# Stack loads in 80 pieces from a scratch in blocks of 512 tokens, issued by SP, and SP's stores placed later behind their data

## The chip, the cores and the metric

The kernel runs on one core of one Trainium2 chip. The core has five engines that run side by side: TensorE (PE, matmuls, with its weight loads shown as PEld), VectorE (DVE), ScalarE (ACT), GpSimd (POOL) and SyncE (SP, which here only issues DMAs). Each engine takes its own instructions in order and waits for others by semaphores. The metric is the device time of one execution in microseconds (us); lower is better.

## The reference

Two results are mixed by a gate that each token computes for itself. One is multi-head attention over 2048 tokens with 32 heads of 20 channels (width 640); the other is the real part of a two-dimensional Fourier transform, written as products with given matrices.

```python
qkv = (x @ wqkv).reshape(B, S, 3, H, Dh)          # S = 2048, H = 32, Dh = 20
scores = einsum("bhqd,bhkd->bhqk", q, k) * Dh ** -0.5
a = einsum("bhqk,bhkd->bhqd", softmax(scores), v) ... @ wo
y = Cr @ (x @ Dr.T) - Ci @ (x @ Di.T)             # seq and hidden DFT matrices
out = g * a + (1 - g) * y                         # g = sigmoid((x * gate_w).sum(-1))
```

All data are float32.

## The kernel before, in words

**Precision.** A float32 operand is split in two parts of a shorter format (`split`, lines 98 to 103: a rounded copy and the rest), and a product is made of three matmuls (`three`). Queries and keys are kept in both parts in a DRAM scratch, `qk_scr`, whose first index is the part, the second the channel (640 of q, 640 of k), the third the token.

**Attention.** Heads go in 16 pairs, and a pair has two *units* of 1024 queries each, so there are 32 units (`NU`). For each pair two tiles are loaded, the *stacks* `kst` and `qst`: for each head 60 rows of 2048 tokens, the parts of its 20 channels stacked so that one matmul of 60 rows sums the three products (key rows: first, second, first part; query rows: first, first, second part). There are two buffers of each stack, by the parity of the pair. Two more rows per head in `qst` hold minus the row maxima of the scores.

A unit takes 32 *steps*, and in each of them PE makes, for both heads, one "m" score (line 159: queries by 512 keys, of which DVE takes the maxima at line 161) and one "e" score (line 685: keys by 512 queries, with the maxima subtracted through the two extra rows, which ACT turns into exponentials at line 687). The m scores run `LEAD` = 41 steps ahead of the e scores. So the maxima of a unit are known about 9 steps before its first e score; then (`max_chain`) PE transposes them, DVE splits them into `m1` and `m2`, and two steps later SP issues four small DMAs that put them into `qst` (lines 201 and 202). The m scores of the next pair begin at step 23 of a pair's 64.

Four steps make a *cycle*, written out by the string `ORDER`: eight e and eight m scores (each for one head), 15 places `F` for filling work, and at its end the *burst* `B`. In the burst PE multiplies the exponentials with `v` (line 448, sixteen matmuls), and DVE and ACT read out finished tiles.

**Filling work.** It is the Fourier transform. First 64 tiles of the product with the hidden matrices (`hid_tile`, lines 301 to 310), 10 of them before the first burst, the others one a cycle; they are stored to `a_scr`. Then, from cycle 57 on, the product with the sequence matrices (`dft_step`, line 523): 56 units of 16 dft steps. For these POOL prepares the operands: it adds or subtracts two tiles of `in_cdft` (line 419) or of `a_scr` (line 433) where a product wants that, and splits them. Results are added into `y_scr` (`finish_y`).

**End of a unit.** The accumulated `av` is copied to `o` by ACT (line 455) and then divided by its sums in seven small stages, each placed a number of steps behind the unit's end: `store_l` and `load_l` bring the sums through DRAM into the tile `lc`, `recip` (DVE, line 468) inverts them, `store_r` and `load_r` spread them over the rows of `rb`, `norm` (POOL, line 478) multiplies, and `store_o` writes `o_scr` (line 486).

**Order.** The program is written in the order of steps, and each engine runs its instructions in that order. `at_step(i, f)` puts a DMA or an instruction at the start of step i (`begin`). SP issues nearly all DMAs from one queue; a DMA that waits for its data holds everything that stands behind it on SP. In program order each SP DMA also waits for the one eight places before it to land. POOL issues the stack loads between its arithmetic: `load_stack(p)` yields twelve DMAs, and `begin` places them two steps apart, from step 2 to step 24 of the pair before. For each head and each of three column ranges (all keys; first and second half of the queries) it makes one DMA of 40 rows, for two stacked parts, and one of 20 rows. Pair 0's stacks are loaded by POOL before the loop (line 357).

Buffers: `raw_tile` has three, shared by the hid tiles' results and the `in_cdft` loads; `o`, `lc` and `rb` have one each; `m1` and `m2` two each.

Of the kernel before, what the change touches and what calls it, by code (L numbers as in the profile page):

```python
# [10 lines left out]
F32 = mybir.dt.float32  # L11
R = mybir.dt.float32r
# [6 lines left out]
P = 128  # L19
S = 2048  # L20
D = 640
H = 32
DH = 20
# [35 lines left out]
def f32(ap):  # L59
    return ap.bitcast(F32)  # L60
# [3 lines left out]
def mix_kernel(ctx: ExitStack, tc: tile.TileContext, xa, wqk, wb, cdft, wo, out):  # L64
# [12 lines left out]
    ps_a = pools(name="ps_a", bufs=1, space=PSUM)  # L77
    ps_y = pools(name="ps_y", bufs=1, space=PSUM)

    qk_scr = dram.tile([2, 2 * D, S], F32, name="qk_scr")  # L80
    v_scr = dram.tile([NP, P, NS, VW], F32, name="v_scr")
    a_scr = dram.tile([2, 2, NS, P, HE], F32, name="a_scr")
    y_scr = dram.tile([NS, P, D], F32, name="y_scr")
# [40 lines left out]
    def v_tile():  # L124
        return work.tile([P, NS, VW], F32, name="v", bufs=2)

    def load_stack(p):
        kt, qt = kst[p % 2], qst[p % 2]
        u = S // 2
        for t, o, two, one, cs in ((kt, D, 0, 2, slice(0, S)), (qt, 0, 1, 0, slice(0, u)), (qt, 0, 1, 0, slice(u, S))):  # L130
            for h in range(2):
                r = (2 * p + h) * DH
                b = 64 * h
                rows = slice(o + r, o + r + DH)
                yield f32(t[b + two * DH : b + (two + 2) * DH, cs]), qk_scr[:, rows, cs]
                yield f32(t[b + one * DH : b + (one + 1) * DH, cs]), qk_scr[0, rows, cs]

    def q_unit(n):
        u = n % 2 * (S // 2)
# [5 lines left out]
    def at_step(i, fn):  # L145
        later.setdefault(i, []).append(fn)
# [43 lines left out]
    def max_chain(n):  # L190
        q = q_unit(n)
        pt = bank()[:16, :P]
        pe.transpose(pt, nms.pop(n), ident)
        m1 = small.tile([16, P], R, name="m1", bufs=2)
        m2 = small.tile([16, P], R, name="m2", bufs=2)
        split(m1, m2, pt, dve, dve)

        def rows():
            for h in range(2):
                b = 64 * h + KROWS  # L200
                sp.dma_start(f32(q[b : b + 1, :]), f32(m1[8 * h : 8 * h + 8, :]))
                sp.dma_start(f32(q[b + 1 : b + 2, :]), f32(m2[8 * h : 8 * h + 8, :]))

        if now[0] < 0:
            rows()
        else:
            at_step(now[0] + 2, rows)
# [49 lines left out]
    def qk_tile(c, t):  # L257
        w = wt[c]
        ps = bank()
        cs = slice(t * 512, (t + 1) * 512)  # L260
        for d in range(ND):
            three(ps, w[:, 0, d], w[:, 1, d], xs[:, 0, d, cs], xs[:, 1, d, cs], d == 0, d == ND - 1)
        st = pair_tile()
        split(st[:, 0].bitcast(R), st[:, 1].bitcast(R), ps, act, dve)
        stores.append((qk_scr[:, c * P : (c + 1) * P, cs].rearrange("z p c -> p z c"), st))
        flush(2)

    def mm_b(j, s, ps, n):
# [137 lines left out]
    def load_c(g):  # L406
        n, j = divmod(g, 2)
        n, t = divmod(n, HT)
        raws = []
        for i, (_, th, ri) in enumerate(PRODUCTS[n][0]):  # L410
            raw = apool[0].tile([P, 1024], F32, name="raw2", bufs=2) if i and apool else raw_tile()
            o = (2 * ri + j) * 1024
            sp.dma_start(raw, cdft[th * HT + t, :, o : o + 1024])
            raws.append(raw)

        def finish():
            c = cparts[g] = part_tile()
            if len(raws) > 1:
                pool.tensor_tensor(raws[0], raws[0], raws[1], op=ALU.add if PRODUCTS[n][0][1][0] > 0 else ALU.subtract)  # L419
            split(c[:, 0], c[:, 1], raws[0], pool, pool)  # L420

        return finish
# [28 lines left out]
            unit_end(i, n)  # L451

    def unit_end(i, n):
        o = pa.tile([P, 512], F32, name="o")
        act.activation(o, av, AF.Copy)
        lc = pa.tile([P, 16], F32, name="lc")
        rb = pa.tile([P, 512], F32, name="rb")

        q = pool if n == NU - 1 else sp

        def store_l():
            q.dma_start(l_scr[n], o.rearrange("(j r) c -> j r c", j=4)[:, DH])

        def load_l():
            q.dma_start(lc, l_scr[n].rearrange("j (a b) -> (j a) b", b=16))

        def recip():
            dve.reciprocal(lc, lc)

        def store_r():  # L470
            q.dma_start(r_scr[n].rearrange("j (a b) -> (j a) b", b=16), lc)

        def load_r():
            for j in range(4):
                q.dma_start(rb[32 * j : 32 * j + 32, :], r_scr[n, j : j + 1].to_broadcast([32, 512]))

        def norm():
            pool.tensor_tensor(o, o, rb, op=ALU.mult)  # L478

        def store_o():  # L480
            for qc in range(2):
                for h in range(2):
                    j = 2 * qc + h
                    t0 = (n % 2) * (S // 2) + qc * 512
                    r = (2 * (n // 2) + h) * DH
                    q.dma_start(o_scr[r : r + DH, t0 : t0 + 512], o[32 * j : 32 * j + DH, :])

        steps = (1, 4, 10, 12, 15, 23, 25) if n < NU - 2 else (1, 4, 10, 12, 15, 19, 21)
        for k, fn in zip(steps, (store_l, load_l, recip, store_r, load_r, norm, store_o)):
            if n == NU - 1:  # L490
                rest.append(fn)
            else:
                at_step(i + k, fn)
# [7 lines left out]
    def dft_step(g):  # L501
        n, t, s = g // NS // HT, g // NS % HT, g % NS
        if s == 0:
            new_y(0), new_y(1)
            outs[n, t] = []
            for _, th, hf in PRODUCTS[n][2]:
                tt = th * HT + t
                y = None
                if (tt, hf) in signs:
                    y = apool[0].tile([P, HE], F32, name="yt", bufs=4)  # L510
                    sp.dma_start(y, y_scr[tt, :, hf * HE : (hf + 1) * HE])
                outs[n, t].append(y)
        if s % 8 == 0 and g // 8 + 3 < 2 * UNITS:
            cfin.append(load_c(g // 8 + 3))
        if s % 8 == 4 and cfin and g // 8 + 2 < 2 * UNITS:
            cfin.pop(0)()
        c = cparts[g // 8]
        cs = slice((s % 8) * P, (s % 8 + 1) * P)
        a = at[n % 2, s]
        for z, (cz, az) in enumerate(((0, 0), (0, 1), (1, 0))):  # L520
            for h in range(2):
                r = slice(64 * h, 64 * h + 64)
                pe.matmul(yp[h][:, :HE], c[r, cz, cs], a[r, az], start=s == 0 and z == 0, stop=s == NS - 1 and z == 2)  # L523
            if z < 2:
                yield
        w = g % (HT * NS) - 16
        if n + 1 == len(PRODUCTS) and w >= 0:
            d, r = divmod(w, 8)
            if r == 0 and d < ND:
                wos[d] = raw_tile()[:, :D]  # L530
                sp.dma_start(wos[d], wo[:, d])
            if r == 5 and d < ND:
                raw = wos.pop(d)
                for h in range(2):
                    wos[d, h] = a_tile(1, 2 * d + h)
                    split(wos[d, h][:, 0], wos[d, h][:, 1], raw[:, h * HE : (h + 1) * HE], pool, pool)
        if s == NS - 1:
            m = apool[0].tile([P, HE], F32, name="m", bufs=2)
            y0, y1 = yp[0][:, :HE], yp[1][:, :HE]

            def read():
                act.activation(m, y0, AF.Copy)
                dve.tensor_tensor(m, y1, m, op=ALU.add)  # L543

            extras.append((now[0], read))
            for out_, y in zip(PRODUCTS[n][2], outs.pop((n, t))):
                extras.append((now[0] + 5, functools.partial(finish_y, out_, t, m, y)))
        yield

    def finish_y(target, t, m, y):  # L550
        sg, th, hf = target
        tt = th * HT + t
        if (tt, hf) in signs:
            pool.tensor_tensor(y, y, m, op=ALU.add if sg == signs[tt, hf] else ALU.subtract)  # L554
        else:
            signs[tt, hf] = sg
            y = m
        at_step(now[0] + 4, functools.partial(sp.dma_start, y_scr[tt, :, hf * HE : (hf + 1) * HE], y))

    preps = []  # L560

# [69 lines left out]
    def begin(i):  # L631
        now[0] = i
        n, s = divmod(i, 32)
        for fn in later.pop(i, ()):
            fn()
        if s % 2 == 0:
            flush()
        if s == 0 and n % 2 == 0:
            p = n // 2
            if p + 1 < NP:  # L640
                at_step(i + 6, functools.partial(load_v, p + 1))
                for j, args in enumerate(load_stack(p + 1)):
                    at_step(i + 2 + 2 * j, functools.partial(pool.dma_start, *args))
        if i < total:
            pts[n, s // 2, s % 2] = pair_tile()

# [145 lines left out]
```

## Time and profile before

| | us |
|---|---|
| three runs | 1954.08, 1959.92, 1956.54 (median 1956.54) |
| the profiled execution's own time | 1953.52 |
| its span, first to last instruction | 1951.7 |
| mean granted TensorE clock | 0.997 of full speed |

A line of the page's groups names the source line, the engine, the operation, what is written and read, and how often; `<-` before an engine or DMA is what ended a wait. "Idle" is the time in which an engine had nothing running just before an instruction. In a list of waits stand the total in us, how many, and the longest. In a timeline stand the start, the length, and in square brackets the idle time before. `SPq` and `POOL ... DMA_DIRECT2D` are the issues of DMAs, not the transfers.

The loop of cycles runs from about 270 us to 1873 us; before it come the projections, after it the output projection and the mix.

### The profile page before, as it was taken

The numbers are of one execution on the slowest core, as the hardware profiler recorded it, in microseconds if no ns is written. First come the engines' busy times: TensorE is split into PE (matmuls) and PEld (weight loads), VectorE is DVE, ScalarE is ACT, GpSimd is POOL, SyncE is SP. The second block draws the span as 40 slices with busy tenths as digits, with TensorE's granted clock in tenths as the row PEclk, the third lists the DMA queues.
The fourth block names the chain that finished last, engine by engine and source line by source line (L and its number), as shares of the span: only waits on it lengthen the run. The fifth ranks groups of instructions, "written<-read, shape, count | busy, mean of one in ns | idle before, by whom it ended". The sixth has DMA issues, their size and how long they took to land. (4 is left out here: it accounts for less than half of the span.)

```text
span 1951.7 us, 43695 instructions
## 1 busy us (share of the span) xinstructions
PE 1918.5 (98%) x17080; PEld 1375.4 (70%) x17080; DVE 1454.1 (75%) x2419; ACT 1211.8 (62%) x2337; POOL 1045.8 (54%) x975
## 2 busy tenths in 40 slices
PE   8999999999999999999999999999999999999999
PEld 7987767777775667666666666666666666666679
DVE  4144568889887888888888878888888887888323
ACT  4221147777776676666776766676766776776741
POOL 1210001111005989457469968995786789787512
PEclk9999999999999999999999999999999999999999
DMA  7763321212114584435356746664554565454355
GB/s 224 173 172 127 130 100 46 78 61 74 47 58 141 170 228 152 122 116 149 97 173 199 196 154 189 212 177 123 149 171 125 183 169 181 154 149 147 98 165 179
DMA packets 196414, 281.02 MB, mean 144 GB/s; under 512 B 73272, under 2 KB 137816, under 8 KB 194288
## 3 DMA queue, kind: packets, MB, share of 16 engines
q1 hardware_dynamic: 158992, 246.20, 40.8%
q0 software_dynamic: 37216, 32.03, 6.7%
q8 instruction: 134, 2.20, 0.5%
q14 instruction: 72, 0.59, 0.1%
HBM read 213.81 MB, written 63.70 MB: 142 GB/s over the span
## 5 line engine op out<-in xcount | busy, mean ns | idle before, releaser
L161 DVE TENSOR_REDUCE mx<-ps 128x1 f32<-128x512 f32 x2048 | 1287.4, 683 | 197.4 <-PE ps L159 178.8
L687 ACT ACTIVATE p<-ps 128x512 f32<-128x512 f32 x2048 | 1080.9, 598 | 443.4 <-PE ps L159 241.2
L159 PE MATMUL ps<-kst,qst 60*128 60x512 f32 x2048 | 776.1, 427 | 8.0 <-DVE mx L161 3.2
L685 PE MATMUL ps<-qst,kst 62*128 62x512 f32 x2048 | 700.7, 422 | 5.8 <-DMA qst<-m 4.2
L523 PE MATMUL yp<-a,part 64*128 64x320 f32 x5376 | 687.6, 309 | 0.1
L523 PEld LDWEIGHTS yp<-a,part 64*128 64x128 f32 x5376 | 593.7, 186 | 15.3 <-DVE m L543 0.3
L448 PE MATMUL av<-p,v 128*21 128x512 f32 x4096 | 494.4, 599 | 0.1
L685 PEld LDWEIGHTS ps<-qst,kst 62*128 62x128 f32 x2048 | 335.5, 185 | 215.2 <-DVE mx L161 181.9
L159 PEld LDWEIGHTS ps<-kst,qst 60*128 60x128 f32 x2048 | 364.5, 185 | 38.2 <-DVE mx L161 11.8
L103 POOL TENSOR_TENSOR part<-raw,part 128x1024 fp32r<-128x1024 f32 x112 | 267.2, 2386 | 9.0
L448 PEld LDWEIGHTS av<-p,v 128*21 128x21 f32 x4096 | 98.3, 100 | 226.8 <-issue 223.1
L301 PE MATMUL yp<-wb,xs 64*128 64x320 f32 x1920 | 237.4, 309 | 3.7 <-ACT raw L309 3.5
L301 PEld LDWEIGHTS yp<-wb,xs 64*128 64x128 f32 x1920 | 206.8, 187 | 8.9 <-ACT raw L309 4.1
L419 POOL TENSOR_TENSOR raw<-raw,raw 128x1024 f32<-128x1024 f32 x78 | 187.4, 2402 | 17.3 <-DMA raw<-in_cdft 11.8
L102 POOL CAST part<-raw 128x1024 fp32r<-128x1024 f32 x112 | 116.4, 1039 | 116.8 <-PE yp L523 87.4
L102 POOL CAST wb<-raw 128x966 fp32r<-128x966 f32 (+1 forms) x4 | 3.4, 856 | 215.8 <-PE ps L159 215.8
L554 POOL TENSOR_TENSOR yt<-yt,m 128x320 f32<-128x320 f32 x64 | 55.5, 878 | 111.3 <-DVE m L543 104.2
L478 POOL TENSOR_TENSOR o<-o,rb 128x512 f32<-128x512 f32 x32 | 41.4, 1294 | 134.5 <-DMA rb<-r_scr 73.7
L103 POOL TENSOR_TENSOR a<-araw,a 128x320 fp32r<-128x320 f32 x112 | 97.8, 873 | 9.0
L103 DVE TENSOR_TENSOR p<-ps,p 128x512 fp32r<-128x512 f32 x40 | 27.5, 691 | 94.1 <-ACT p L100 91.4
L106 PE MATMUL ps<-xs,part 128*128 128x512 f32 x200 | 80.2, 401 | 7.8 <-ACT xs L100 6.1
L100 ACT ACTIVATE p<-ps 128x512 fp32r<-128x512 f32 x40 | 23.7, 597 | 101.4 <-PE ps L108 101.4
(67 smaller groups left out, 1331.8 us busy)
## 6 DMA issues: line engine op xcount, KB each, us to landing
raw<-in_cdft SPq DMA_DIRECT2D x192, 512.0 KB
araw<-a_scr SPq DMA_DIRECT2D x192, 160.0 KB
qk_scr<-p SPq DMA_DIRECT2D x40, 512.0 KB
kst<-qk_scr POOLq DMA_DIRECT2D x32, 320.0 KB, 12.3
qst<-qk_scr POOLq DMA_DIRECT2D x64, 160.0 KB, 8.2
a_scr<-raw SPq DMA_DIRECT2D x64, 160.0 KB
yt<-y_scr SPq DMA_DIRECT2D x64, 160.0 KB
y_scr<-yt SPq DMA_DIRECT2D x64, 160.0 KB
```

The source lines that it names most:

```text
L102: e1.tensor_copy(dst1, src)
L103: e2.tensor_tensor(dst2, src, f32(dst1), op=ALU.subtract)
L106: pe.matmul(ps, st1, mv1, start=first, stop=False)
L159: pe.matmul(ps, q[b : b + KROWS, qt * P : (qt + 1) * P], k[b : b + KROWS, kc * 512 : (kc + 1) * 512], start=True, stop=True)
L161: return lambda: dve.tensor_reduce(mx[n][:, h, qt, kc : kc + 1], ps, axis=AX.X, op=ALU.max)
L301: pe.matmul(yp[h][:, :HE], xs[r, xz, d, cs], w[r, wz, d, :HE], start=d == 0 and z == 0, stop=d == ND - 1 and z == 2)
L419: pool.tensor_tensor(raws[0], raws[0], raws[1], op=ALU.add if PRODUCTS[n][0][1][0] > 0 else ALU.subtract)
L448: pe.matmul(av[32 * j : 32 * j + DH + 1, :], v[:, kt, h * (DH + 1) : (h + 1) * (DH + 1)], pp[qc][:, h, :], start=kt == 0, stop=kt == NS - 1)
L523: pe.matmul(yp[h][:, :HE], c[r, cz, cs], a[r, az], start=s == 0 and z == 0, stop=s == NS - 1 and z == 2)
L554: pool.tensor_tensor(y, y, m, op=ALU.add if sg == signs[tt, hf] else ALU.subtract)
L685: pe.matmul(pt, k[b : b + KROWS + 2, kt * P : (kt + 1) * P], q[b : b + KROWS + 2, qc * 512 : (qc + 1) * 512], start=True, stop=True)
L687: act.activation(pts[n, kt, qc][:, h], pt, AF.Exp, scale=float(DH) ** -0.5)
```

## The change

The scratch of queries and keys is laid out in blocks of 512 tokens, so that what one `qk_tile` stores is contiguous for each part. A stack is loaded in six DMAs, one for each head and each of the three stacked parts, of 20 rows by four blocks of 512 tokens (80 pieces of 2 KB each); queries are no longer loaded in halves. There are twelve such DMAs for a pair as before. Inside the loop they are issued by SP at steps 2 to 13 of the pair before, one a step; POOL still issues those of pair 0.

The seven stages at the end of a unit are placed later (the last two units keep their places), and `o` gets a second buffer; the store of `y_scr` comes eight steps behind the addition instead of four; the loads of `y_scr` come at dft step 8 of a unit, behind the `in_cdft` load of the same step, instead of at dft step 0 ahead of it. `m1` and `m2` have one buffer each instead of two.

```diff
-    qk_scr = dram.tile([2, 2 * D, S], F32, name="qk_scr")
+    qk_scr = dram.tile([2, 4, 2 * D, 512], F32, name="qk_scr")
...
     def load_stack(p):
-        kt, qt = kst[p % 2], qst[p % 2]
-        u = S // 2
-        for t, o, two, one, cs in ((kt, D, 0, 2, slice(0, S)), (qt, 0, 1, 0, slice(0, u)), (qt, 0, 1, 0, slice(u, S))):
+        for t, o, parts in ((kst[p % 2], D, (0, 1, 0)), (qst[p % 2], 0, (0, 0, 1))):
             for h in range(2):
-                r = (2 * p + h) * DH
-                b = 64 * h
-                rows = slice(o + r, o + r + DH)
-                yield f32(t[b + two * DH : b + (two + 2) * DH, cs]), qk_scr[:, rows, cs]
-                yield f32(t[b + one * DH : b + (one + 1) * DH, cs]), qk_scr[0, rows, cs]
+                r = o + (2 * p + h) * DH
+                for k, z in enumerate(parts):
+                    b = 64 * h + k * DH
+                    yield (f32(t[b : b + DH, :]).rearrange("r (t c) -> r t c", t=4),
+                           qk_scr[z, :, r : r + DH, :].rearrange("t r c -> r t c"))
...
-        m1 = small.tile([16, P], R, name="m1", bufs=2)
-        m2 = small.tile([16, P], R, name="m2", bufs=2)
+        m1 = small.tile([16, P], R, name="m1")
+        m2 = small.tile([16, P], R, name="m2")
...
-        stores.append((qk_scr[:, c * P : (c + 1) * P, cs].rearrange("z p c -> p z c"), st))
+        stores.append((qk_scr[:, t, c * P : (c + 1) * P].rearrange("z p c -> p z c"), st))
...
-        o = pa.tile([P, 512], F32, name="o")
+        o = pa.tile([P, 512], F32, name="o", bufs=2)
...
-        steps = (1, 4, 10, 12, 15, 23, 25) if n < NU - 2 else (1, 4, 10, 12, 15, 19, 21)
+        steps = (6, 10, 16, 23, 27, 34, 45) if n < NU - 2 else (1, 4, 10, 12, 15, 19, 21)
...
         if s == 0:
             new_y(0), new_y(1)
             outs[n, t] = []
+        if s % 8 == 0 and g // 8 + 3 < 2 * UNITS:
+            cfin.append(load_c(g // 8 + 3))
+        if s % 8 == 4 and cfin and g // 8 + 2 < 2 * UNITS:
+            cfin.pop(0)()
+        if s == 8:
             for _, th, hf in PRODUCTS[n][2]:
...
-        if s % 8 == 0 and g // 8 + 3 < 2 * UNITS:
-            cfin.append(load_c(g // 8 + 3))
-        if s % 8 == 4 and cfin and g // 8 + 2 < 2 * UNITS:
-            cfin.pop(0)()
...
-        at_step(now[0] + 4, functools.partial(sp.dma_start, y_scr[tt, :, hf * HE : (hf + 1) * HE], y))
+        at_step(now[0] + 8, functools.partial(sp.dma_start, y_scr[tt, :, hf * HE : (hf + 1) * HE], y))
...
                 for j, args in enumerate(load_stack(p + 1)):
-                    at_step(i + 2 + 2 * j, functools.partial(pool.dma_start, *args))
+                    at_step(i + 2 + j, functools.partial(sp.dma_start, *args))
```

## The prediction

> **What bounds the kernel now.** I read the page's head first, then the waits of PE, then PE's timeline by its marker, the sixteen `av` matmuls (L448) that close every cycle of four steps.
>
> ```profile
> span 1951.7 us, 43695 instructions
> ...
> PE 1918.5 (98%) x17080; PEld 1375.4 (70%) x17080; DVE 1454.1 (75%) x2419; ACT 1211.8 (62%) x2337; POOL 1045.8 (54%) x975
> ```
> ```profile
> PE ps L685 <- DMA qst<-m: 4.2, 2, 3.3
> ...
> PE ps L159 <- DMA qst<-qk_scr: 2.4, 1, 2.4
> ```
>
> PE is busy 98% of the span, and no store, no cdft load and no POOL product ever holds it. A transfer reaches PE in two ways only: through the stacks (`qst<-qk_scr`) and through the two rows of maxima (`qst<-m`). So the change can win only what these waits cost, with what hangs on them, and lose only where it makes a new one. The price of a wait is read from the distance of `av` bursts:
>
> ```profile
> 1124.88 1.91 PE L448 MATMUL av<-p,v 128*21 128x512 f32 x16
> ...
> 1133.93 0.89 PE L685 MATMUL ps<-qst,kst 62*128 62x512 f32 x2 [3.28 <-DMA qst<-m]
> 1134.75 3.01 PE L448 MATMUL av<-p,v 128*21 128x512 f32 x16
> ...
> 1142.02 1.91 PE L448 MATMUL av<-p,v 128*21 128x512 f32 x16
> 1148.12 1.91 PE L448 MATMUL av<-p,v 128*21 128x512 f32 x16
> 1154.44 1.92 PE L448 MATMUL av<-p,v 128*21 128x512 f32 x16
> ```
>
> From 1142.02 on two cycles take 12.42 us, so an undisturbed cycle is 6.21 and a step 1.55. The two cycles before took 17.14: **place A costs 4.7 us**, of which 3.28 is the wait; the rest is a slower PE behind it (its next burst 3.01 instead of 1.91).
>
> Why were the rows late? DVE had them ready; SP sends them in its order:
>
> ```profile
> 1121.05 0.28 DVE L103 TENSOR_TENSOR m<-ps,m 16x128 fp32r<-16x128 f32 x1
> ...
> 1114.39 0.38 SPq L635 DMA_DIRECT2D y_scr<-m  x1
> 1124.67 1.42 SPq L486 DMA_DIRECT2D o_scr<-o  x4
> ...
> 1127.83 0.68 SPq L201 DMA_DIRECT2D qst<-m  x1
> ...
> 1122.69 0.64 POOL L635 DMA_DIRECT2D qst<-qk_scr  x1
> 1123.34 1.30 POOL L478 TENSOR_TENSOR o<-o,rb 128x512 f32<-128x512 f32 x1
> ```
>
> SP issued nothing from 1114.8 to 1124.67: it stood at the store of `o`, which waited for POOL's `norm` (L478, done 1124.6), itself behind a stack DMA that POOL issues. The rows, ready at 1121.3, left at 1127.83. Place B is the same with the other transfer in front:
>
> ```profile
> 1615.00 1.91 PE L448 MATMUL av<-p,v 128*21 128x512 f32 x16
> 1622.04 0.76 PE L159 MATMUL ps<-kst,qst 60*128 60x512 f32 x1 [2.40 <-DMA qst<-qk_scr]
> 1624.69 2.10 PE L448 MATMUL av<-p,v 128*21 128x512 f32 x16
> ...
> 1637.89 0.77 PE L685 MATMUL ps<-qst,kst 62*128 62x512 f32 x2 [0.95 <-DMA qst<-m]
> 1638.59 1.91 PE L448 MATMUL av<-p,v 128*21 128x512 f32 x16
> ...
> 1613.42 1.15 POOL L635 DMA_DIRECT2D qst<-qk_scr  x2
> 1616.88 1.15 POOL L635 DMA_DIRECT2D qst<-qk_scr  x2
> ```
>
> Three cycles took 23.59 instead of 18.63: **place B costs 5.0 us**. POOL had come late to its stack DMAs (1613 to 1618, where PE wanted the first half at 1619.6). Place C goes through DVE, which stood before the reciprocal of `lc`:
>
> ```profile
> 892.90 1.91 PE L448 MATMUL av<-p,v 128*21 128x512 f32 x16
> 900.49 1.92 PE L448 MATMUL av<-p,v 128*21 128x512 f32 x16
> ...
> 897.94 0.25 DVE L468 RECIPROCAL lc<-lc 128x16 f32<-128x16 f32 x1 [1.33 <-DMA lc<-l_scr]
> ...
> 886.53 0.32 SPq L465 DMA_DIRECT2D lc<-l_scr  x1
> ```
>
> One cycle of 7.59: **place C costs 1.4 us**. The little `lc` load took 11.4 us to land, in the steps where the stack DMAs run.
>
> **The change part by part.** SP's own waits show what its queue is made of:
>
> ```profile
> SPq L462 <- ACT p L687: 166.8, 29, 9.2
> SPq L471 <- DVE lc L468: 149.5, 28, 10.4
> ...
> SPq L486 <- POOL o L478: 108.0, 25, 14.9
> ```
>
> *The later steps* (6, 10, 16, 23, 27, 34, 45 after a unit's end, y stores 8 instead of 4 steps behind). `store_l` now comes 5 steps (7.8 us) later than before, against a mean wait of 5.8 (166.8/29); `store_r` keeps 7 steps behind the reciprocal instead of 2, and `store_o` 11 behind `norm` instead of 2, that is 17 us where the longest wait was 14.9. So these 424 us of waits mostly go. Only what stands behind them counts: the rows of maxima at step 26 no longer have `store_o` (25) before them but `store_r` (23), long due. Place A returns, and the second wait in B. The second `o` buffer is what lets `store_o` reach past the next unit's end; `m1` and `m2` with one buffer are rewritten 32 steps later, and cost nothing.
>
> *The stack DMAs* move from POOL's steps 2 to 24 to SP's 2 to 13. The m-scores of the next pair begin 23 steps into a pair (LEAD 41 of 64), so the last one has 10 steps, 15.5 us, to land. What did they take?
>
> ```profile
> kst<-qk_scr POOLq DMA_DIRECT2D x32, 320.0 KB, 12.3
> qst<-qk_scr POOLq DMA_DIRECT2D x64, 160.0 KB, 8.2
> ...
> L201 SPq DMA_DIRECT2D qst<-m x64: 634/648/780, 233.8 to 1829.1; - x64
> ...
> L486 SPq DMA_DIRECT2D o_scr<-o x124: 277/325/1522, 356.7 to 1855.7; - x124
> ```
>
> Even at 12.3 us they are in time, so the first wait in B returns. SP's issue of a 20x4x512 piece is not in the trace: between 0.33 (20 rows) and 0.65 us (the slow form), 4 to 8 us a pair of 99 us. I take 0.5, nearer to the 20-row store; it lies in the time that SP stood waiting, and were that used up, SP would run late by those 8 us, still inside 15.5. The first of them waits for PE's last e-score of the pair before, two steps earlier in program order; behind it stand SP's araw and cdft loads, which POOL wants 12 us later. POOL loses 12 issues a pair, which hides behind PE either way.
>
> The 80 pieces of 2 KB carry the same bytes. [...]
>
> *The order of y and cdft loads* at a unit's start: y now comes 8 dft steps later, half a unit (11 us) before its use by POOL. No cost while the half unit before POOL's use covers it; were that used up, POOL would wait, and PE not before POOL were a part behind.
>
> *The head.* Pair 0's stacks stay on POOL. There its ninth issue waited for the first to land, and the memset of `v` behind it held ACT and then PE:
>
> ```profile
> 73.05 1.19 POOL L357 DMA_DIRECT2D qst<-qk_scr  x2 [8.72 <-DMA kst<-qk_scr]
> ...
> 70.00:80.00 10.00, 7.36 (x50) 7.09 (x50) 0.56 (x1) 2.16 (x5) 3.57 (x6) 1.00 0.59 170
> ```
>
> PE lost 2.6 us in that stretch. Smaller first copies land earlier or not: 0 to 2.6 gained, I take 1.3.
>
> *From the hid tiles to the dft* two waits of ACT pass to PE:
>
> ```profile
> 596.05 0.44 ACT L309 ACTIVATE raw<-yp 128x320 f32<-128x320 f32 x1 [1.52 <-POOL raw L419]
> ...
> 611.93 0.44 ACT L309 ACTIVATE raw<-yp 128x320 f32<-128x320 f32 x1 [3.37 <-POOL raw L419]
> ```
>
> They hang on two cdft loads at steps 202 and 210, where SP now also issues pair 4's stacks (194 to 205) while POOL no longer does. The first may land later, the second earlier: between 4.9 gained and 4.9 lost, I take 0.
>
> *The new risk* is the `lc` load: its step 10 lies among the stack DMAs, and DVE's reciprocal stands 6 steps (9.3 us) behind it, as before. Bounds: 0, and place C's 1.4 at each of 15 pair starts, 21 us. I take one, 1.4, since before, with the same 6 steps, it happened once (the 8.7 of the next rows is after the last m-score, where DVE has time).
>
> ```profile
> DVE lc L468 <- DMA lc<-l_scr: 10.3, 3, 8.7
> ...
> 686.00:707.00 21.00, 21.00 (x209) 14.25 (x211) 17.88 (x30) 14.70 (x28) 16.90 (x21) 1.00 0.99 259
> ```
>
> **The sum**, against the profiled execution's own 1953.5 (span 1951.7 and 1.8 around it): minus 4.7, 5.0 and 1.4, minus 1.3, plus 1.4, gives 1942.5. That execution is 3.0 under the median of the runs shown, 1956.54, and these spread over 5.8. I can't see how much of that is waits of this kind, and go to the middle of 1942.5 and 1945.5: **1944 us**.
>
> [...]
>
> **The rivals.**
> *The waits only move* (chance 0.18). SP stays one queue, and its araw and cdft loads wait for buffers that POOL frees; in a heavy product POOL runs 6.6 us behind (`norm` at step 23 lies 9 steps, 14 us, before the first e-score of the next unit, wanted at 1130.65, so it was due at 1116.7 and ran at 1123.34). A late POOL then holds the rows through a load instead of a store. For it: SP had such waits already. Against it: the loads ask for buffers given back a cycle earlier, the store asked for work 2 steps old. If A and B come back: 1944 + 9.7 = 1953.7, no change.
>
> *Slower: DVE waits at every pair start* (0.15). Twelve stack DMAs in 17 us instead of 34, in one queue with `lc`. In the quoted 21 us of a pair start the DMA engines are 0.99 busy at 259 GB/s, and a stack is 1.92 MB, 7.4 us at that rate. It decides once `lc` takes over 9.3 us, and 11.4 was seen once. Price: 15 times 1.4, in place of the one in my sum: 1944 + 19.6 = 1963.6. Against it: only one of 15 pair starts had it, with POOL's DMAs running just then.
>
> *The change doesn't do what it says* (0.03): stacks land after step 23 because SP is late. Then B's wait recurs and eats A's gain, 1956.
>
> **Chances and range.** My forecast has 0.64, with a range of its own of 1939 to 1950. A measurement of this kernel can tell about 0.3%, 5.9 us: faster is below 1950.6, slower above 1962.4. Faster: 0.64 and a little of the first rival, 0.65; the same 0.19; slower 0.16, the second rival and a little. The range for 8 in 10 leaves out the slower rival (0.15) and a twentieth below: 1938, where the head and half of the 4.9 are won as well, to 1959.
>
> **What would show it.** Right: no wait of PE for `qst<-m` or `qst<-qk_scr`, L462, L471 and L486 gone from SP's waits, all DFT cycles between 6.1 and 6.5 us, and PE's clock at 1.00 there. Wrong: waits of DVE for `lc` at pair starts (second rival), PE waits at L685 or L159 with SP standing before L413 or L428 (first), a longer wait at L309 between 590 and 620.

## The result, and the profile after

The changed kernel takes **1933.69 us**, median of 6 runs (1931.83 to 1935.72); beside it the kernel before took 1960.32 (6 runs, 1954.08 to 1967.25). The ratio is 0.9869, 95% interval 0.9852 to 0.9885: faster by 1.3%. The profiled execution took 1935.29, 18.2 us less than that of before. Forecast were 1944 and a range of 1938 to 1959: the direction was right, the gain too small by half.

The page's head after, with PE's waits. The same PE work stands in a span that is 18.2 us shorter; both DMA rows (`qst<-m`, `qst<-qk_scr`) are gone, and so is the wait for `v` in the head.

```profile
span 1933.5 us, 43647 instructions
...
PE 1914.5 (99%) x17080; PEld 1374.1 (71%) x17080; DVE 1456.7 (75%) x2419; ACT 1211.5 (63%) x2337; POOL 944.3 (49%) x795
...
PE ps L106 <- ACT xs L100: 6.3, 1, 6.3
PE ps L158 <- DVE mx L160: 1.7, 2, 0.8
PE ps L106 <- ACT part L100: 1.3, 1, 1.3
```

PE's timeline after by its marker, first where place A was, then place B. The distances are 6.31, 6.09 and 6.17, then 6.13, 6.29 and 6.10: undisturbed cycles.

```profile
1111.38 1.92 PE L447 MATMUL av<-p,v 128*21 128x512 f32 x16
1117.69 1.91 PE L447 MATMUL av<-p,v 128*21 128x512 f32 x16
1123.78 1.92 PE L447 MATMUL av<-p,v 128*21 128x512 f32 x16
1129.95 1.91 PE L447 MATMUL av<-p,v 128*21 128x512 f32 x16
...
1602.20 1.91 PE L447 MATMUL av<-p,v 128*21 128x512 f32 x16
1608.33 1.92 PE L447 MATMUL av<-p,v 128*21 128x512 f32 x16
1614.62 1.92 PE L447 MATMUL av<-p,v 128*21 128x512 f32 x16
1620.72 1.92 PE L447 MATMUL av<-p,v 128*21 128x512 f32 x16
```

SP's own waits after: the longest sum is now at the rows of maxima, where SP is early and waits for DVE, as it should. What stood in its queue before, at the stores of `l`, `lc` and `o`, has fallen from 166.8, 149.5 and 108.0 to 52.7, 106.8 and 8.5.

```profile
SPq L200 <- DVE m L103: 253.5, 32, 13.3
...
SPq L470 <- DVE lc L467: 106.8, 19, 15.4
...
SPq L461 <- ACT p L687: 52.7, 22, 6.0
...
SPq L412 <- POOL raw L418: 35.3, 20, 5.9
SPq L427 <- POOL araw L432: 33.2, 17, 4.0
...
SPq L485 <- POOL o L477: 8.5, 1, 8.5
```

Where the 18.2 us came from, by the starts of the `av` bursts (256 cycles, numbered from 0; all numbers in us). "Before" was profiled four times in all, the first being the one that the prediction read; the other kernels are those of the experiments below.

| | before, four executions | after | places alone | stacks alone | store of `o` alone |
|---|---|---|---|---|---|
| span | 1951.7, 1951.9, 1954.1, 1956.3 | 1933.5 | 1933.7 | 1932.3 | 1949.6 |
| start of the first burst (head) | 279.1, 280.2, 280.6, 280.4 | 276.6 | 278.9 | 275.4 | 281.3 |
| cycles 48 to 63 (hid tiles to dft) | 106.6, 106.6, 109.3, 109.1 | 104.1 | 99.7 | 102.5 | 107.1 |
| cycles 96 to 103 (place C) | 51.2, 50.8, 50.3, 50.0 | 49.7 | 49.7 | 49.8 | 50.0 |
| cycles 128 to 135 (place A) | 54.6, 53.7, 52.4, 53.9 | 49.7 | 49.7 | 49.8 | 49.7 |
| cycles 208 to 215 (place B) | 55.2, 54.8, 56.0, 56.5 | 49.9 | 51.6 | 50.1 | 55.4 |

Against the first execution of before, from unrounded times: A 4.96, B 5.34 and C 1.49, together 11.8; the head 2.5; hid tiles to dft 2.5; and 1.5 in all other cycles, mostly the second cycle of each unit, which took 6.17 or more and takes 6.09 now. Its median is 6.09 to 6.10 in every run with the later places and still 6.17 with the stacks alone, so it belongs to the places; what shortens it is not known.

In the head the trace shows why. A line of a stretch has the time and the length, then the busy time and count of PE, PEld, DVE, ACT and POOL, the clock, the DMA share and GB/s. The window in which PE lost 2.6 us is full (before it held 7.36 busy), because POOL waits 3.6 us in short pieces for the first stack copies instead of 8.72 at one, and the memset of `v` behind them runs at 70.64 instead of 75.99. The other runs agree: where the stacks are loaded by copies of 20 rows, the first burst starts between 275.4 and 277.2, and where they are loaded by the old copies, between 278.9 and 281.3.

```profile
70.00:80.00 10.00, 10.00 (x70) 10.00 (x69) 0.83 (x1) 2.28 (x5) 1.91 (x3) 1.00 1.01 208
```
```profile
65.17 0.58 POOL L356 DMA_DIRECT2D qst<-qk_scr  x1 [0.48 <-DMA kst<-qk_scr]
66.39 0.58 POOL L356 DMA_DIRECT2D qst<-qk_scr  x1 [0.64 <-DMA kst<-qk_scr]
68.46 0.58 POOL L356 DMA_DIRECT2D qst<-qk_scr  x1 [1.49 <-DMA kst<-qk_scr]
70.06 0.58 POOL L356 DMA_DIRECT2D qst<-qk_scr  x1 [1.02 <-DMA kst<-qk_scr]
70.64 0.68 POOL L275 MEMSET v<- 128x672 f32 x1
```

From the hid tiles to the dft, SP's queue tells it, first of before, then of after. Before, the first pair of cdft loads stood behind `lc`'s load, which left 8.4 us behind the store of `l`, for whose landing it waited. That load now comes six steps later, and the cdft pair leaves at 581.93 instead of 587.28 and the next at 596.21 instead of 599.61 (of which 2.5 is the head).

```profile
576.87 0.54 SPq L462 DMA_DIRECT2D l_scr<-o  x1
585.24 0.31 SPq L465 DMA_DIRECT2D lc<-l_scr  x1
...
587.28 0.88 SPq L413 DMA_DIRECT2D raw<-in_cdft  x2
...
599.61 1.50 SPq L413 DMA_DIRECT2D raw<-in_cdft  x2
```
```profile
581.93 0.91 SPq L412 DMA_DIRECT2D raw<-in_cdft  x2
...
596.21 0.83 SPq L412 DMA_DIRECT2D raw<-in_cdft  x2
```

From issue to the start of POOL's work on it, the first pair takes longer now (8.3 us instead of 6.4), but the second, which had held PE longest, takes 5.6 instead of 10.0. It took 9.8 to 10.8 in all four executions of before and with the store of `o` alone, where POOL's old stack copies and the loads of `rb` are issued beside it; it takes 6.3 with the places alone, where `rb` comes later, and 6.1 with the stacks alone, where POOL issues no copies.

So the later places are not the only cure. With the stacks alone, where `lc`'s load kept its old place, it leaves 1.9 us behind the store, and cycles 48 to 63 take 102.5; with the store of `o` alone, where the old copies and the old place of that load stay, they take 107.1.

```profile
573.37 0.55 SPq L460 DMA_DIRECT2D l_scr<-o  x1
...
575.29 0.35 SPq L463 DMA_DIRECT2D lc<-l_scr  x1
```

The 2.5 us are a net gain: cycle 52 fell from 9.64 to 6.29, while cycle 54 rose from 6.07 to 7.65 through a lower clock (0.63, then 0.52; last section).

### The profile page after: what moved, and what is told of

Same layout as the page of the kernel before. It is cut to its first block, busy times and chain, and to the rows that moved or that the text cites. A ratio compares the mean times of both kernels' runs of the same rounds, so it can differ in the third digit from the quotient of the medians.

```text
span 1933.5 us, 43647 instructions
## 1 busy us (share of the span) xinstructions
PE 1914.5 (99%) x17080; PEld 1374.1 (71%) x17080; DVE 1456.7 (75%) x2419; ACT 1211.5 (63%) x2337; POOL 944.3 (49%) x795
## 5 line engine op out<-in xcount | busy, mean ns | idle before, releaser
L554 POOL TENSOR_TENSOR yt<-yt,m 128x320 f32<-128x320 f32 x64 | 55.4, 877 | 135.4 <-DVE m L543 128.3
```

## The experiments

**The places alone.** The changed kernel with the old scratch and the old 2 x 20-row and 20-row copies, issued by POOL at steps 2 to 24:

```diff
-                    at_step(i + 2 + j, functools.partial(sp.dma_start, *args))
+                    at_step(i + 2 + 2 * j, functools.partial(pool.dma_start, *args))
...
-    qk_scr = dram.tile([2, 4, 2 * D, 512], F32, name="qk_scr")
+    qk_scr = dram.tile([2, 2 * D, S], F32, name="qk_scr")
```

> The later places, the second o buffer and the y order of the change, with the stacks and their scratch as before (POOL, steps 2 to 24). If the gain of 26.6 us (1960.3 to 1933.7) comes from SP no longer standing before stores: 1938 to 1944, with no wait of PE for qst<-m, but head and hid-to-dft as before (first av burst near 279 us, a cycle of over 9 us between 600 and 615). If it comes from the stack transfers: 1950 to 1957.

Measured: 1937.06 us (1933.83 to 1942.65), ratio 0.9908 (0.9892 to 0.9925). A is gone. Of B its first wait is left, with one cycle of 7.90 (PE's timeline), and the head stays at 278.9.

```profile
1606.61 0.47 PE L160 MATMUL ps<-kst,qst 60*128 60x512 f32 x1 [1.58 <-DMA qst<-qk_scr]
```

**The stacks alone.** The kernel before with the new scratch and its 20x4x512 copies, issued by SP at steps 2 to 13; the old places and buffers stay.

> The scratch in blocks and the twelve loads of 20x4x512 from SP at steps 2 to 13, with all places of stores as before. If SP's standing before stores is the cause: 1950 to 1957, SP's waits at the store of o and at l_scr still over 80 us each, and late stacks or rows on PE. If the stack transfers are the cause: 1936 to 1942, first av burst near 276.6 us, no cycle over 9 us.

Measured: 1934.21 us (1933.86 to 1935.26), ratio 0.9887 (0.9875 to 0.9900). A, B and C are all gone, although the store of `o` still stands ahead of the rows. At place A POOL, which issues no stacks now, runs `norm` in time, and SP gets through (first POOL, then SP):

```profile
1109.78 1.29 POOL L476 TENSOR_TENSOR o<-o,rb 128x512 f32<-128x512 f32 x1
```
```profile
1111.10 3.08 SPq L484 DMA_DIRECT2D o_scr<-o  x4
...
1115.61 0.68 SPq L199 DMA_DIRECT2D qst<-m  x1
```

So the two parts overlap: savings of 19 and 22 us against the 1956.25 us that before took in that series, and no 41 together. This run changes both the shape of the copies and the engine that issues them; which of the two cures A at the old places was not tried.

**POOL issues the new copies.** The changed kernel, with `pool` in place of `sp` at `at_step(i + 2 + j, ...)`.

> All of the change, but POOL issues the twelve pieces of a pair, at the same steps 2 to 13. If only order on SP and the pieces' shape matter: 1933 to 1937, as with SP. If POOL's lateness in heavy products is what made stacks late: PE waits for qst<-qk_scr at pairs near 1100 and 1590 us, 1938 to 1948.

Measured: 1933.35 us (1932.75 to 1934.66), ratio 0.9883 (0.9870 to 0.9896). With these copies and the later places, it makes no difference which engine issues. Here the page shows the landing of all the new copies, from the key stacks' row and the query stacks':

```profile
kst<-qk_scr POOLq DMA_DIRECT2D x96, 160.0 KB, 6.3
qst<-qk_scr POOLq DMA_DIRECT2D x96, 160.0 KB, 7.9
```

**SP issues the old copies.** The changed kernel with the old scratch and the old copies, but on SP at steps 2 to 13.

> All of the change, but the scratch and the pieces as before (40 and 20 rows, queries in halves), issued by SP at steps 2 to 13. If the pieces' shape does not matter: 1933 to 1937. If the 40-row pieces run on few DMA engines and delay what stands beside them: 1938 to 1950, with the first av burst back near 279 us, DVE waiting for lc at pair starts or PE waiting for stacks.

Measured: **2090.48 us** (2086.92 to 2093.60), ratio 1.0685 (1.0667 to 1.0702). This is the prediction's slower rival in full size. The waits of DVE, PE and SP:

```profile
DVE lc L469 <- DMA lc<-l_scr: 128.8, 14, 12.6
```
```profile
PE ps L687 <- DVE mx L162: 63.2, 9, 10.4
PE yp L525 <- DVE m L545: 31.5, 3, 11.8
```
```profile
SPq L637 <- DMA kst<-qk_scr: 102.7, 31, 8.4
```

DVE stands at the reciprocal 14 times, 9.2 us in the mean (128.8/14), and PE behind it. Per pair of 15 the kernel loses 10.2 us ((2086.0 - 1933.5)/15), of which 0.3 is the later first burst.

**The same, with rows of 8 KB in copies of 20.** As the last one, but each copy loads 20 rows at full width from one part, as the changed kernel does. Beside the old scratch, the edit against the changed kernel is:

```diff
-                    yield (f32(t[b : b + DH, :]).rearrange("r (t c) -> r t c", t=4),
-                           qk_scr[z, :, r : r + DH, :].rearrange("t r c -> r t c"))
+                    yield f32(t[b : b + DH, :]), qk_scr[z, r : r + DH, :]
```

> The changed kernel, but with the old scratch layout: SP still issues twelve stack copies of 20 rows at steps 2 to 13, each row one run of 8 KB now instead of four of 2 KB. It tells the shape of a copy (20 rows in one level against 2 x 20 rows) from its pieces of 2 KB. Theory 1 (a copy of 2 x 20 rows is moved by few DMA engines and so lands late, and holds what is queued behind it; one whose slowest level has 20 rows is not): as the changed kernel, 1930 to 1938 us, stack copies landing in 6 to 8 us, and no wait of DVE for lc at pair starts. Theory 2 (the pieces of 2 KB in blocks of 512 tokens are what shortened the landing): as the kernel with 40-row copies on SP, 2050 to 2100 us, with DVE waiting for lc about 9 us at most pair starts.

Measured: 1935.27 us (1934.68 to 1939.04), ratio 0.9885 (0.9865 to 0.9905). The layout in blocks of 512 tokens and the 80 pieces are not what helps: this kernel has the old layout, is not told apart from the changed one, and stands 155 us below the last. The two differ only in how a stack is cut: there, six of the twelve copies of a pair go over both parts in one (and the queries in halves). What that does shows in stretches in which nearly all packets were rows of 8 KB, those of the stacks, first of the last kernel, then of this one:

```profile
498.00:500.00 2.00, 2.00 (x27) 1.95 (x25) 1.97 (x4) 1.85 (x4) 0.00 (x0) 1.00 0.13 53
500.00:502.00 2.00, 2.00 (x25) 1.71 (x26) 1.96 (x4) 1.41 (x4) 0.00 (x0) 1.00 0.13 53
```
```profile
476.00:478.00 2.00, 2.00 (x25) 1.89 (x21) 1.94 (x4) 1.57 (x4) 0.00 (x0) 1.00 0.68 176
```

A share of 0.13 is as much as two of the 16 DMA engines at work all the time, and 0.68 as much as about eleven. The six copies carry 1,280 KB a pair (two of 320 and four of 160); at 53 GB/s they need some 25 us, an estimate, where steps 2 to 13 are 17, and the load of `lc` is issued among them. No row names the engines, and why 53 GB/s moved in the first two stretches and 176 in the third is not shown.

How much of the harm is SP's and how much the faster pace is open: the places alone took 1937.06 us with the same copies, but there POOL issued them over steps 2 to 24, and SP was not tried at that pace.

**The store of `o` alone.** The kernel before with two edits that belong together:

```diff
-        o = pa.tile([P, 512], F32, name="o")
+        o = pa.tile([P, 512], F32, name="o", bufs=2)
...
-        steps = (1, 4, 10, 12, 15, 23, 25) if n < NU - 2 else (1, 4, 10, 12, 15, 19, 21)
+        steps = (1, 4, 10, 12, 15, 23, 45) if n < NU - 2 else (1, 4, 10, 12, 15, 19, 21)
```

> The kernel before, with one edit: the store of o at step 45 after a unit's end instead of 25, and the second buffer of o that this needs. The old scratch and the 40-row copies on POOL stay. If place A was the rows of maxima standing behind the store of o on SP, as the prediction read it, the wait of PE for qst<-m at cycles 128 to 135 goes and these eight cycles take 49.7 us instead of 54.6; place B keeps its first wait (qst<-qk_scr, 2.4 us) and loses its second (0.95), C keeps its 1.4, and head and hid tiles are as before: 4.7 + 1.0 less than the kernel before, a ratio of about 0.997. If the rows were late through the stack copies instead, the wait stays and the ratio is 1.000. If most of the gain of the later places comes from this one store (they alone gave 0.9908), the ratio is 0.991 to 0.993.

Measured: 1950.54 us (1945.87 to 1953.83), ratio 0.9961 (0.9949 to 0.9974), with before at 1957.71. A is gone (49.7), B is not (55.4, with a first wait of 3.83 us). This shows A's cause as the prediction read it: POOL's `norm` is as late as ever, and the rows of maxima leave 2.4 us before it, instead of behind it (SP, then POOL):

```profile
1122.76 0.68 SPq L201 DMA_DIRECT2D qst<-m  x1
```
```profile
1125.20 1.30 POOL L478 TENSOR_TENSOR o<-o,rb 128x512 f32<-128x512 f32 x1
```

**Before, three times more.**

> The kernel before, unchanged, for a second profiled execution. Its times ran from 1952 to 1967 us, those of the changed kernel from 1932 to 1936. If this spread is waits of the kind of A, B and C that come and go from one execution to the next, this trace shows the same kinds of waits at other units, and their cycles account for its difference from 1953.5 us. If the spread lies elsewhere (the clock, the ends of the span), A, B and C stand at the same cycles with the same lengths.

> The kernel before, unchanged, for one more profiled execution. In its 17 runs of the second series the time falls by 1.8 us for each 0.001 of mean granted clock (0.990 at 1964.94, 0.996 at 1953.41); two profiled executions, both near the short end, showed A, B and C at the same cycles. If a longer execution (over 1957) comes up and its extra time is a lower clock: the same waits of PE as in the first, with cycles at clock 0.83 in more places. If it is more waits: waits of PE for DMA well over 6.6 us in sum.

> The same as the one before it: the kernel before, unchanged, for a fourth profiled execution, to see where its time differs from the others. Expected if the clock is the cause: cycles with waits take longer than the wait in them, at clock 0.83, and the longer the execution the more of those; if more waits: waits of PE for DMA well over 6.6 us in sum.

Measured: 1953.65, 1958.07 and 1955.91 us. All four executions have A, B and the hid tiles' stalls at the same cycles (the table above; C in parts). The longest, 1956.3 of span, has its extra 4.6 us mostly there: 2.5 from the hid tiles to the dft, 1.4 in the head, 1.3 in B, and 1.4 in cycles 144 to 151, where the rows of maxima were late a third time; 0.8 and 1.1 less in A and C. PE's waits for DMA in it are 8.0 us, against 6.6 in the first:

```profile
PE ps L685 <- DMA qst<-m: 5.7, 3, 2.3
...
PE ps L159 <- DMA qst<-qk_scr: 2.3, 1, 2.3
```

So most of what varies is waits at the places that the prediction found, and the slower PE behind them (in the longest the burst behind A's wait of 2.30 us took 3.30 instead of 1.91). Executions over 1960 were not profiled, and stay open.

**The dft one cycle sooner.** After the change some cycles between hid tiles and dft are still long, so this was tried to beat it: the changed kernel with `first = start // 4 + 2` in place of 3.

> The changed kernel, with the dft starting one cycle sooner after the hid tiles (start // 4 + 2 instead of + 3), so that one cycle less runs without fills. Theory 1 (what is left of the slow cycles 50 to 56 is the empty cycles: PE idles behind ACT there and its clock falls to 0.83 at 630 to 640 us): one of the long cycles at 54 to 56 (7.7 against 6.2) goes, 1.0 to 3 us less than the changed kernel, 1931 to 1933. Theory 2 (the wait for POOL's raw, which waits for the in_cdft load, sets the place): the same loads are wanted a cycle sooner, the waits of ACT at L308 grow by as much, and the time is that of the changed kernel or up to 3 us more.

Measured: 1939.69 us (1937.73 to 1942.11), ratio 0.9905 (0.9885 to 0.9925). One 7.73 cycle became 6.32 as theory 1 has it, but the next takes 11.52: PE waits for POOL's `a`, because POOL works on without a gap (none over 0.1 us from 619.9 to 652.7) and can't be ready sooner. POOL sets that place, at another of its tiles than theory 2 said.

```profile
644.61 0.63 PE L523 MATMUL yp<-a,part 64*128 64x320 f32 x2 [2.53 <-POOL a L102]
```

**The cdft loads one cycle sooner.**

```diff
-            if c in (HID - 5, HID - 3):
-                at_step(i + 4, load_c((c - HID + 5) // 2))
+            if c in (HID - 6, HID - 4):
+                at_step(i + 8, load_c((c - HID + 6) // 2))
```

> The changed kernel, with the first two pairs of cdft loads issued one cycle (6.2 us) sooner on SP, and POOL's work on them left where it is. Theory 1 (between the hid tiles and the dft the changed kernel still waits because these loads land late: ACT stands at L308 for POOL's raw at 592.6, and cycle 50 takes 7.31): cycle 50 goes to 6.25, and cycles 48 to 63 together lose 1 to 4 us of their 104.1, 1930 to 1933 us. Theory 2 (the three raw buffers are the limit: two of them are held a cycle longer, so ACT stands there as long, or longer): cycles 48 to 63 take 104 us or more, and the time is that of the changed kernel or up to 3 us above it.

Measured: 1932.35 us (1930.26 to 1933.36), ratio 0.9875 (0.9856 to 0.9893); span 1930.5. Cycle 50 went from 7.31 to 6.24, and cycles 48 to 63 from 104.1 to 102.9: in this one execution it goes as theory 1 has it, with 1.2 us. Cycle 50 differs from run to run without this edit too (6.25 where POOL issues the new copies, 8.19 with rows of 8 KB). It is the shortest median of all kernels here, but its interval covers that of the changed kernel: not shown to be better.

## Why the prediction was right or wrong

The causes at A, B and C were read rightly, and the gain came out twice as large as forecast because the terms beside them were too small. The largest of these, the cycles from the hid tiles to the dft, was put at 0 and measured 2.5.

**Places A, B and C: right.** The sum took off 4.7, 5.0 and 1.4; 11.8 went against the same execution. "Place A returns" is shown for the later store by the store of `o` alone; what the prediction missed is that the new copies, issued by SP at the old places, return A as well, so A had two sufficient cures. For B's first wait the stack copies were named rightly: with places alone 1.58 us of it stays. C varies between 0.4 and 1.5 us over the four executions, and is 0.3 with the store of `o` alone; the sum took its high end from one execution, and what cures it is not settled. No run shows why its 1.4 should go, as the sum has it; the runs showed cycles 96 to 103 at 49.7 after the change and with the places alone, at 49.8 with the stacks alone and at 50.0 with the store of `o` alone, against 50.0 to 51.2 before. Two of the signs named for being right did not hold in full, without a cost: of the 424 us that SP stood at the three stores, 168 are left, most of them at the store of `lc` (106.8 us, longest 15.4), and single dft cycles still take 6.5 to 6.8 us.

**"Even at 12.3 us they are in time": true only with the change's own copies.** Twelve old copies on SP cost 153 us of span. The prediction weighed them as so many KB in one queue (7.4 us at 259 GB/s), and put the risk on the new copies, which by the runs are the safe ones (1934.21 us where SP issues them at the old places, 1933.69 in the change). The slower rival's mechanism, place and deciding point (an `lc` load over 9.3 us) were right; its cause was the shape of the copy, not the number in one queue. Its price of 1.4 for each pair start was taken from one mild case, and was 10.2 where it struck.

**The head: mis-sized.** 1.3 taken from 0 to 2.6; 2.5 measured, and against the four executions of before 3.5 (mean 280.1 against 276.6).

**From the hid tiles to the dft: this step failed.** "The first may land later, the second earlier ... I take 0": it measured 2.5 gained, and 3.8 against the four executions. The two directions were right for the landing (1.9 us longer for the first pair, 4.4 shorter for the second), but they were set off against each other to nothing. The reasoning also left out that the wait for `l`'s store, which held the first pair's issue, goes: by the prediction's own later steps, and, as the stacks alone show, by the new copies too. The opening had put the place aside already ("no cdft load and no POOL product ever holds it"), though the list of PE's waits before has it:

```profile
PE yp L301 <- ACT raw L309: 3.5, 2, 2.7
```

After the change 0.3 is left of it.

**The `lc` risk: 1.4 that did not come.** DVE waits for `lc` once, 8.6 us in the tail, as before.

**The rest.** SP's issue of a 20x4x512 piece was taken as 0.5 us and has a median of 0.33 (keys) and 0.30 (queries). The 1.5 us of slightly shorter cycles elsewhere were not named.

**The addition.** The sum of 1942.5 stands against 1935.29 of the same kind of execution: 7.2 too much, made of 0.7 in the places, 1.2 in the head, 2.5 at the hid tiles, 1.4 for `lc`, and 1.5 not named (7.3, less 0.1 at the ends). Another 1.5 came from "go to the middle", and 1.6 from the changed kernel's profile standing over its median. That step to the middle went the wrong way. In the four profiled executions of before, what varied was for the most part waits that the change takes away, so a longer execution of before would mean a larger gain, and not a longer time after. This is argued from the spreads, not shown: the changed kernel's runs spread over 3.9 us, those of before beside it over 13.2. **The range** was cut where it should not have been: the far ends of its own bounds (head 2.6, hid tiles 4.9, no `lc`) give 1942.5 - 1.3 - 4.9 - 1.4 = 1934.9, and 1938 left them out. The profiled execution lies within that; the median of 1933.69 is still 1.2 below it.

**The rival that waits only move** did not happen: SP now stands 35.3 us before L412 and 33.2 before L427 for POOL, and no row of maxima is late through it.

## What to carry to other kernels

When several terms of a sum are waits of one kind (a queue standing before something late), a change that takes the cause away can take them all, also those that vary from run to run: the spread of the old kernel may then be part of the gain, not noise around it. Before a copy moves to another queue, look at how it is cut: here copies of two parts of 20 rows each, issued by SP one a step, took 155 us more than copies of one part, while issued by POOL every second step they took under 4 us more (1937.06 against 1933.35). Where two edits cure one wait, run each alone before either is given the credit.

## What the runs showed of the hardware that was not expected

PE's clock fell to 0.52 with hardly a gap in PE's work. Stretches of 2 us of the changed kernel between hid tiles and dft, where no wait of PE is over 0.31 us (from 600 to 645 us):

```profile
608.00:610.00 2.00, 2.00 (x26) 1.91 (x23) 1.89 (x4) 1.75 (x4) 0.00 (x0) 1.00 0.04 8
...
614.00:616.00 2.00, 2.00 (x9) 1.14 (x7) 2.00 (x4) 2.00 (x5) 0.00 (x0) 1.00 0.06 11
616.00:618.00 2.00, 2.00 (x12) 0.65 (x14) 1.94 (x4) 1.11 (x3) 0.00 (x0) 0.63 0.61 174
618.00:620.00 2.00, 2.00 (x12) 0.18 (x4) 0.00 (x0) 0.00 (x0) 1.78 (x4) 0.52 0.69 166
```

The clock goes to 0.52 behind 9 matmuls in 2 us, where 26 stand in the first line: PE's work was thin there, and its busy time full (2.00 of 2.00). With the places alone the same stretch of the program is as thin, and the clock stays:

```profile
614.00:616.00 2.00, 1.99 (x9) 1.07 (x7) 2.00 (x5) 1.99 (x5) 0.00 (x0) 1.00 0.32 107
616.00:618.00 2.00, 2.00 (x11) 1.01 (x14) 2.00 (x4) 1.42 (x4) 0.00 (x0) 1.00 0.13 23
```

From execution to execution of the kernels here these cycles without fills cost between 0 and 3 us: with the places alone none of cycles 53 to 58 is over 6.5, after the change two of them take 7.65 and 7.73. A sum from one execution could not show that. Why the clock fell in the one execution and stayed in the other is not shown.
